# Products with v in groups of five and four key tiles, with eleven exponential buffers and three running sums

## The chip, the cores and the metric

The kernel runs on one core of a Trainium2 chip. The metric is the device time of one execution in microseconds (us), as the median of several runs. The core has a matrix engine (TensorE, PE in the rows; its weight loads are PEld), a vector engine (VectorE, DVE), a scalar engine (ScalarE, ACT), GpSimd (POOL) and a queue that issues DMAs (SyncE, SP). They run side by side and wait for each other through semaphores.

## What is computed

Attention with queries pooled in pairs, then two dense stages with their own weights. The weights come as 64-bit floats, read as pairs of integers and converted on the chip; the rest is float32.

```
q_pool = q.reshape(B, H, S // 2, 2, D).mean(axis=3)      # B, H, S, D = 4, 8, 1152, 64
scores = scale * np.matmul(q_pool, k.transpose(0, 1, 3, 2))
scores = scores - np.max(scores, axis=-1, keepdims=True)
attn = np.exp(scores)
attn = attn / (np.sum(attn, axis=-1, keepdims=True) + 1e-09)
x = np.matmul(attn, v)                                   # then (B*S/2, H*D) = (2304, 512)
h = x @ w_in;  x = (h - np.tanh(h)) @ w_out              # 512 -> 2048 -> 512
h = x @ w_in2; r = np.maximum(h, 0); out = (s * r * r + b) @ w_out2
```

## The kernel before

Heads are taken in pairs: `pairs` counts 16 of them, n = 0 to 15, four for each of the four batches, and j = 0 or 1 is the head within the pair. The 1152 keys of a head are 9 tiles of 128, t = 0 to 8. The 576 pooled queries are two halves of 288, g = 0 or 1.

For each key tile, `scores` makes two products for each half (L454 with 128 rows, L455 with 65 rows, which adds the row of maxima) into one of two PSUM buffers `s`, and ScalarE's exponential (L456) writes the half into a tile `pf` of 128 x 576. There are `PFB` buffers of `pf`. Each finished tile goes to the list `pend`. From n = 4 on, GpSimd adds the `pf` tiles of a head into a running sum `acc` (L517), two program steps after the tile is made, and when more than `BATCH` = 3 tiles are pending, `batch` multiplies the three oldest with v (L558): two halves side by side, each with 64 columns of the array, into PSUM `pv`. At the last batch of a head, one tile into the next head, `total` multiplies the running sum with ones (L572) into `su`, in the same block. The last head, (15, 1), has no running sum on GpSimd: `sum_plain` sums with ones on TensorE (L496).

A planner (the scheduler of the framework) sets the order of instructions on every engine ahead of time from priorities and its own costs; within an engine they run in that order. `batch` runs at a high priority (`AHEAD` = 400) and after the latest score product, so its products stand together in one block. Around the scores the planner puts the preparation of later pairs (transposes ptq L357, ptk L376, ptc L420; products ptm L415, whose maxima VectorE takes in L416) and the first dense stage of earlier batches (`sweep1`: h L626, y L639). These go to four PSUM buffers. During the last pair, VectorE and GpSimd also convert the weights w6 to w8 for the next stage (L215 to L239), since buffers become free there; tha and gla are VectorE's operations of the gate between h and y.

A head of nine tiles has these batches: tiles 0 to 2 when tile 3 is made, 3 to 5 at tile 6, 6 to 8 at tile 0 of the next head.

Of the kernel before, what the change touches and what calls it, by code (L numbers as in the profile page):

```python
# [46 lines left out]
GROUPS_LAST = ((0, 1, 2, 3, 4), (5, 6, 7, 8))  # L47
BATCH = 3
STORE, PUT = 8, 6
# [3 lines left out]
AHEAD = 400  # L53
PFB = 10
SOON = 40
# [8 lines left out]
def attention_moe_moe_kernel(  # L64
# [418 lines left out]

    def sum_plain(n, j, t0):


        if t0 == 0:
            return
        if (n, j) not in sums:
            sums[n, j] = psV.tile([P, HB], F32, tag="su", name=f"su{n}_{j}")  # L490
        su = sums[n, j]
        while fresh and fresh[0][:2] == (n, j) and fresh[0][2] < t0 + BATCH:
            _, _, u, pf = fresh.pop(0)
            for g in range(2):
                o = 32 * (2 * (u % 2) + g)
                mm(su[o:o + 32], ones[:, 0:32], pf[:, g * HB:(g + 1) * HB],  # L496
                   start=(u < 2), stop=(u >= NKT - 2))
        if t0 == NKT - BATCH:
            later(1, lambda: spread_plain(n, j))
# [12 lines left out]
    def add(n, j, t, r, pf):  # L512

        old = accs[n, j, r]
        if t == groups(n, j)[r][1]:
            accs[n, j, r] = ap.tile([P, SQ], F32, tag="acc", name=f"acc{n}_{j}_{r}", bufs=4)
        added[0] = pool.tensor_add(accs[n, j, r], old, pf)  # L517
# [14 lines left out]
    def finish_single(n, j):  # L532
# [12 lines left out]
        later(2, total)  # L545

    def batch():


        todo = [pend.popleft() for _ in range(BATCH)]  # L550
        n, j, t, _ = todo[0]
        if t == 0:
            pvt[n, j] = psV.tile([P, HB], F32, tag="pv", name=f"pv{n}_{j}")
        po = pvt[n, j]
        with tc.high_priority(offset=AHEAD), tc.issue_after(last[0].ins):
            for i, (_, _, u, pf) in enumerate(reversed(todo)):
                for g in (1, 0):
                    mm(po[g * D:(g + 1) * D], vos[j][:, u, 0:D], pf[:, g * HB:(g + 1) * HB],  # L558
                       start=(t == 0 and i == 0), stop=(u == NKT - BATCH))
            total()  # L560
            if plain(n, j):
                sum_plain(n, j, t)
        if t == NKT - BATCH:
            later(0, lambda: finish_head(n, j))
# [147 lines left out]
    for n in range(len(pairs)):  # L712
# [3 lines left out]
        for j in range(2):  # L716
            for t in range(NKT):
# [22 lines left out]
                else:  # L740
                    tick()
                    if len(pend) > BATCH:
                        batch()
# [363 lines left out]
```

## Time and profile before

| | us |
|---|---|
| median of 3 runs | 1344.11 |
| lowest and highest run | 1339.24, 1345.49 |
| profiled execution, device time | 1338.49 |
| span of its instructions | 1336.7 |
| TensorE busy in the span | 1307.3 (98%) |
| VectorE, ScalarE, GpSimd busy | 947.2, 634.4, 347.7 |

A row of a timeline gives start, length, engine, line, operation, result <- operands and how many records are merged; in brackets stands how long the engine was idle before it and what ended that. Records of TensorE overlap: products are pipelined, a record of 0.29 us is followed by the next start after about 0.13 us. So what a product costs the stream is the distance to the next start, not the length of its record. [...]

### The profile page before, as it was taken

How to read it: one execution, taken by the hardware profiler on the slowest of the kernel's cores; microseconds unless marked ns; L12 is line 12 of the kernel's file. 1: busy time of each engine (PE TensorE's matmuls, PEld its weight loads, DVE VectorE, ACT ScalarE, POOL GpSimd, SP SyncE). 2: the span in 40 equal slices, each digit the busy share in tenths (PEclk: the TensorE clock that was granted, in tenths of full speed). 3: DMA queues.
4: the chain of work that ended last, by engine and by line, in shares of the span. 5: the costliest groups of instructions: out<-in, count | busy, mean ns of one | idle time of the engine just before them, and what ended most of it. 6: DMA issues, size and time to landing. Idle time of an engine off the chain costs nothing.

```text
span 1336.7 us, 22381 instructions
## 1 busy us (share of the span) xinstructions
PE 1307.3 (98%) x8118; PEld 1125.2 (84%) x8118; DVE 947.2 (71%) x1888; ACT 634.4 (47%) x1527; POOL 347.7 (26%) x287
## 2 busy tenths in 40 slices
PE   6999999999999999998999999999999999999998
PEld 4777767777887777876999999999988888889887
DVE  6988885857575665668788577676878787655654
ACT  2455555555565555654333333333445454444532
POOL 0222257766677767763000000000000000000000
PEclk9999999999999999999999999999999999999999
DMA  8777766675657566443786224457434274404031
GB/s 178 160 180 179 177 153 135 143 186 133 165 112 175 129 147 156 112 119 120 239 271 193 68 82 137 147 181 245 133 118 150 95 228 153 147 0 142 1 95 48
DMA packets 203183, 191.61 MB, mean 143 GB/s; under 512 B 88640, under 2 KB 170688, under 8 KB 203072
## 3 DMA queue, kind: packets, MB, share of 16 engines
q1 hardware_dynamic: 200736, 189.59, 52.7%
q8 instruction: 64, 1.05, 0.3%
q10 hardware_dynamic: 2336, 0.59, 0.2%
q14 instruction: 47, 0.39, 0.1%
HBM read 115.34 MB, written 39.32 MB: 116 GB/s over the span
## 4 chain that ended last, share of the span: by engine, by line
PE 90%; DVE 5%; DMA 3%; ACT 1%; issue 1%; SPq 1%; POOL 0%; DVEq 0%; ACTq 0%; POOLq 0%
PE o L987 15%; PE y L828 11%; PE h L817 11%; PE pv L558 8%; PE h L1032 8%; PE s L454 6%; PE k L1032 6%; PE s L455 5%; PE ptm L415 5%; PE y L639 4%; PE h L626 3%; PE pv L526 2%; PE su L526 2%; PE ptk L376 1%; DVE mp L416 1%
## 5 line engine op out<-in xcount | busy, mean ns | idle before, releaser
L456 ACT ACTIVATE pf<-s 128x288 f32<-128x288 f32 x576 | 223.6, 410 | 161.5 <-PE s L455 156.5
L416 DVE TENSOR_REDUCE mp<-ptm 128x1 f32<-128x384 f32 x384 | 202.5, 544 | 104.5 <-PE ptm L415 100.0
L517 POOL TENSOR_TENSOR acc<-acc,pf 128x576 f32<-128x576 f32 x159 | 228.1, 1434 | 53.2 <-ACT pf L456 44.7
L454 PE MATMUL s<-U,T 128*128 128x288 f32 x576 | 191.9, 338 | 1.6 <-ACT pf L456 1.0
L455 PE MATMUL s<-U,T 65*128 65x288 f32 x576 | 172.8, 304 | 0.0
L828 PE MATMUL y<-ghb,w 128*128 128x288 f32 x784 | 171.9, 295 | 0.2 <-DVE yr L836 0.2
L817 PE MATMUL h<-xx,w 128*128 128x288 f32 x1176 | 171.0, 294 | 1.0 <-DMA xx<-x1d 0.6
L817 PEld LDWEIGHTS h<-xx,w 128*128 128x128 f32 x1176 | 160.6, 188 | 1.5 <-DMA xx<-x1d 0.9
L987 PE MATMUL o<-w,g2h 128*128 128x512 f32 x486 | 154.7, 394 | 0.0
L415 PE MATMUL ptm<-T,U 128*128 128x384 f32 x360 | 135.7, 383 | 2.7 <-DVE mp L416 1.9
L454 PEld LDWEIGHTS s<-U,T 128*128 128x128 f32 x576 | 109.9, 191 | 25.8 <-ACT pf L456 10.9
L828 PEld LDWEIGHTS y<-ghb,w 128*128 128x128 f32 x784 | 131.3, 188 | 0.4 <-DVE yr L836 0.4
L558 PE MATMUL pv<-pf,vo 128*64 128x288 f32 x864 | 120.7, 415 | 0.0
L455 PEld LDWEIGHTS s<-U,T 65*128 65x128 f32 x576 | 110.4, 192 | 7.1 <-issue 4.4
L828 PE MATMUL y<-glb,w 128*128 128x288 f32 x392 | 116.0, 296 | 0.0
L1032 PE MATMUL h<-w,w 128*128 128x384 f32 x522 | 107.4, 339 | 0.0
L1032 PEld LDWEIGHTS h<-w,w 128*128 128x128 f32 x522 | 93.6, 188 | 9.4 <-DVE w L902 1.1
L987 PEld LDWEIGHTS o<-w,g2h 128*128 128x128 f32 x486 | 89.7, 187 | 10.0
L987 PE MATMUL o<-w,g2l 128*128 128x512 f32 x234 | 92.6, 396 | 0.0
L558 PEld LDWEIGHTS pv<-pf,vo 128*64 128x64 f32 x864 | 55.6, 136 | 41.0 <-issue 10.8
L950 ACT ACTIVATE r_c<-r_c 128x384 f32<-128x384 f32 x72 | 37.8, 524 | 109.5 <-DVE r_c L1044 53.1
L955 DVE SCALAR_TENSOR_TENSOR g2l<-r_c,sb,g2h 128x384 fp32r<-128x384 f32 x96 | 59.1, 616 | 39.7 <-ACT g2h L954 39.4
(145 smaller groups left out, 2369.4 us busy)
## 6 DMA issues: line engine op xcount, KB each, us to landing
xx<-x1d SPq DMA_DIRECT2D x80, 288.0 KB
T<-T SPq DMA_DIRECT2D x50, 288.0 KB
raw<-in_moe_w_in_dram SPq DMA_DIRECT2D x23, 512.0 KB
raw<-in_moe_w_out_dram SPq DMA_DIRECT2D x23, 512.0 KB
qr<-in_q_dram SPq DMA_DIRECT2D x32, 288.0 KB
vo<-in_v_dram SPq DMA_DIRECT2D x32, 288.0 KB
x1d<-xo SPq DMA_DIRECT2D x64, 144.0 KB
kr<-in_k_dram SPq DMA_DIRECT2D x30, 288.0 KB
```

What stands on the lines that cost most here:

```text
L415: mm(pt, U1[j][:, q0:q0 + P], T1[j][:, kk], start=True, stop=True)
L416: newest[0] = dve.reduce_max(mp[:, s, i:i + 1], pt, axis=AX.X)
L454: last[0] = mm(ps, T1[j][:, t * P:(t + 1) * P], U1[j][:, sl], start=True, stop=False)
L455: last[0] = mm(ps, T2[j][:, t * P:(t + 1) * P], U2[j][:, sl], start=False, stop=True)
L456: act(pf[:, sl], ps, AF.Exp, scale=SCALE)
L517: added[0] = pool.tensor_add(accs[n, j, r], old, pf)
L558: mm(po[g * D:(g + 1) * D], vos[j][:, u, 0:D], pf[:, g * HB:(g + 1) * HB], start=(t == 0 and i == 0), stop=(u == NKT - BATCH))
L817: mm(ps[:, :n], w[:, a, c * P:(c + 1) * P], xx[:, c, x, 0:n], start=(i == 0 and c == 0), stop=(i == 2 and c == NDC - 1))
L828: mm(ys[i][c], w[:, a, c * P:(c + 1) * P], x, start=(f == fa and r == 0), stop=(f == fb - 1 and r == 2))
L955: gates.append(dve.scalar_tensor_tensor(out=gl, in0=r, scalar=sb2[:, 1:2], in1=f32(gh), op0=ALU.add, op1=ALU.subtract))
L987: mm(os[r], g[:, k * P:(k + 1) * P], w[a], start=(first and n == half and x == 0), stop=(last and n != half and x == 2))
L1032: mm(ps, u[a][:, (2 * wa + c) * P:(2 * wa + c + 1) * P], xs[b][xa][:, c], start=(fresh_ and h == 0 and c == 0), stop=(h == 2 and c == 1), ...
```

## The change

`BATCH` is replaced by `SPLIT` = (5, 4): a head's tiles 0 to 4 are multiplied with v when tile 5 is made, tiles 5 to 8 at tile 0 of the next head. The last head keeps three threes (`SPLIT_LAST`). `PFB` goes from 10 to 11, and the running sums from 4 buffers to 3, each of the same size, so the memory in use is the same. The sums over keys in the last head are unchanged.

```
-BATCH = 3
+SPLIT = (5, 4)
+SPLIT_LAST = (3, 3, 3)
-PFB = 10
+PFB = 11
...
-            accs[n, j, r] = ap.tile([P, SQ], F32, tag="acc", name=f"acc{n}_{j}_{r}", bufs=4)
+            accs[n, j, r] = ap.tile([P, SQ], F32, tag="acc", name=f"acc{n}_{j}_{r}", bufs=3)
...
+    def size(n, j, t):
+
+        split = SPLIT_LAST if plain(n, j) else SPLIT
+        return split[[sum(split[:i]) for i in range(len(split))].index(t)]
+
     def batch():
-        todo = [pend.popleft() for _ in range(BATCH)]
-        n, j, t, _ = todo[0]
+        n, j, t, _ = pend[0]
+        todo = [pend.popleft() for _ in range(size(n, j, t))]
+        closing = todo[-1][2] == NKT - 1
...
-                       start=(t == 0 and i == 0), stop=(u == NKT - BATCH))
+                       start=(t == 0 and i == 0), stop=(closing and i == len(todo) - 1))
...
-                    if len(pend) > BATCH:
+                    if len(pend) > size(*pend[0][:3]):
                         batch()
```

The planner makes new orders of all engines from this. In TensorE's order the products with v and the sums behind them stand in 72 unbroken blocks before and in 49 now. Right behind a block stands a ptc transpose 4 times before and 18 times now. Line numbers of the changed kernel are higher by 1 ahead of `batch` and by 7 behind it.

The score product of a half k+2 writes the buffer of half k. How many other products (not scores) stand between half k's last product and half k+2's first, in attention from pair 4 on, is this:

| other products between | 0 | 1 | 2 | 3 | 4 or more | a block with v |
|---|---|---|---|---|---|---|
| places before | 15 | 10 | 39 | 64 | 168 | 132 |
| places now | 36 | 22 | 50 | 54 | 180 | 86 |

TensorE around the first block of head (7, 1), before: s is a score product, pv a product with v, h the first dense stage, ptm a maximum's product.

```order
L626 MATMUL h0_1_2_3699<-xx0_1_3522,w2_152 128x288
L454 MATMUL s7_1_3_0_3748<-U1_1_1_179,T1_1_1_173 128x288
L455 MATMUL s7_1_3_0_3748<-U2_1_195,T2_1_169 128x288
L415 MATMUL ptm8_0_3_0_3752<-T1_2_0_174,U1_2_0_180 128x384
L626 MATMUL h0_1_2_3699<-xx0_1_3522,w2_152 128x288
L454 MATMUL s7_1_3_1_3756<-U1_1_1_179,T1_1_1_173 128x288
L455 MATMUL s7_1_3_1_3756<-U2_1_195,T2_1_169 128x288
L558 MATMUL pv7_1_3765<-pf7_1_2_3723,vo1_191 64x288 x2
L558 MATMUL pv7_1_3765<-pf7_1_1_3701,vo1_191 64x288 x2
L558 MATMUL pv7_1_3765<-pf7_1_0_3662,vo1_191 64x288 x2
L626 MATMUL h0_1_2_3699<-xx0_1_3522,w2_152 128x288
L415 MATMUL ptm8_0_3_1_3761<-T1_2_0_174,U1_2_0_180 128x384
```

Now, the same head's first block, on TensorE:

```order
L455 MATMUL s7_1_4_1_3778<-U1_1_1_179,T1_1_1_173 128x288
L456 MATMUL s7_1_4_1_3778<-U2_1_195,T2_1_169 128x288
L455 MATMUL s7_1_5_0_3805<-U1_1_1_179,T1_1_1_173 128x288
L456 MATMUL s7_1_5_0_3805<-U2_1_195,T2_1_169 128x288
L455 MATMUL s7_1_5_1_3817<-U1_1_1_179,T1_1_1_173 128x288
L456 MATMUL s7_1_5_1_3817<-U2_1_195,T2_1_169 128x288
L565 MATMUL pv7_1_3833<-pf7_1_4_3766,vo1_191 64x288 x2
L565 MATMUL pv7_1_3833<-pf7_1_3_3747,vo1_191 64x288 x2
L565 MATMUL pv7_1_3833<-pf7_1_2_3723,vo1_191 64x288 x2
L565 MATMUL pv7_1_3833<-pf7_1_1_3701,vo1_191 64x288 x2
L565 MATMUL pv7_1_3833<-pf7_1_0_3660,vo1_191 64x288 x2
L421 MATMUL ptc8_0_3785<-ident_75,m8_0_3634 5x128
```

The block comes two tiles later and is longer, the score products ahead of it stand next to each other, and a ptc transpose has moved right behind it.

GpSimd near the end of head (15, 0), before: acc is the running sum, w the subtraction that ends a weight's conversion.

```order
L239 TENSOR_TENSOR w6_7439<-t0_6_0_0_7442,w6_7439 128x256
L239 TENSOR_TENSOR w6_7439<-t0_6_0_1_7462,w6_7439 128x256
L517 TENSOR_TENSOR acc15_0_1_7498<-pf15_0_5_7450,pf15_0_6_7470 128x576
L517 TENSOR_TENSOR acc15_0_1_7498<-acc15_0_1_7498,pf15_0_7_7509 128x576
L239 TENSOR_TENSOR w7_7440<-t0_7_0_0_7501,w7_7440 128x256
L517 TENSOR_TENSOR acc15_0_1_7498<-acc15_0_1_7498,pf15_0_8_7532 128x576
```

Now, GpSimd at the same place:

```order
L518 TENSOR_TENSOR acc15_0_1_7496<-pf15_0_5_7443,pf15_0_6_7474 128x576
L240 TENSOR_TENSOR w6_7432<-t0_6_0_0_7435,w6_7432 128x256
L240 TENSOR_TENSOR w6_7432<-t0_6_0_1_7466,w6_7432 128x256
L518 TENSOR_TENSOR acc15_0_1_7496<-acc15_0_1_7496,pf15_0_7_7507 128x576
L518 TENSOR_TENSOR acc15_0_1_7496<-acc15_0_1_7496,pf15_0_8_7530 128x576
L240 TENSOR_TENSOR w7_7433<-t0_7_0_0_7499,w7_7433 128x256
```

The last addition, of tile 8, has moved ahead of the subtraction for w7.

VectorE at the end of the last head, before: t and raw are the last weight's conversion, ri and xv the last head's division, tha and gla the last gate of the sweep.

```order
L215 TENSOR_SCALAR t0_8_1_1_7764<-raw0_8_1_1_7720 128x256
L218 SCALAR_TENSOR_TENSOR t0_8_1_1_7764<-raw0_8_1_1_7720,t0_8_1_1_7764 128x256
L592 RECIPROCAL ri15_1_7819<-ri15_1_7819 128x144
L221 SCALAR_TENSOR_TENSOR t0_8_1_1_7764<-raw0_8_1_1_7720,t0_8_1_1_7764 128x256
L224 TENSOR_SCALAR raw0_8_1_1_7720<-raw0_8_1_1_7720 128x256
L592 RECIPROCAL ri15_1_7819<-ri15_1_7819 128x144
L227 SCALAR_TENSOR_TENSOR t0_8_1_1_7764<-raw0_8_1_1_7720,t0_8_1_1_7764 128x256
L653 TENSOR_TENSOR tha2_1_4_7873<-h2_1_4_7801,tha2_1_4_7873 128x288
L597 TENSOR_TENSOR xv15_1_7823<-xv15_1_7823,ri15_1_7819 128x288
L657 TENSOR_TENSOR gla2_1_4_7877<-tha2_1_4_7873,gha2_1_4_7876 128x288
```

Now, VectorE at the same place:

```order
L216 TENSOR_SCALAR t0_8_1_1_7764<-raw0_8_1_1_7720 128x256
L660 TENSOR_TENSOR tha2_1_4_7873<-h2_1_4_7801,tha2_1_4_7873 128x288
L219 SCALAR_TENSOR_TENSOR t0_8_1_1_7764<-raw0_8_1_1_7720,t0_8_1_1_7764 128x256
L604 TENSOR_TENSOR xv15_1_7823<-xv15_1_7823,ri15_1_7819 128x288
L222 SCALAR_TENSOR_TENSOR t0_8_1_1_7764<-raw0_8_1_1_7720,t0_8_1_1_7764 128x256
L225 TENSOR_SCALAR raw0_8_1_1_7720<-raw0_8_1_1_7720 128x256
L664 TENSOR_TENSOR gla2_1_4_7877<-tha2_1_4_7873,gha2_1_4_7876 128x288
L228 SCALAR_TENSOR_TENSOR t0_8_1_1_7764<-raw0_8_1_1_7720,t0_8_1_1_7764 128x256
```

Both reciprocals now stand further ahead, tha ahead of four operations of the conversion, and gla behind three of them. At the start of the same stretch, tha2_1_0 now stands ahead of the two casts of w6, which stood ahead of it before. In SyncE's order the load of the last weight part, raw0_8_1_1, now stands behind the first load of xx0, the next stage's input, instead of ahead of it.

## Rows read from the trace of the kernel before

**Rows 1.** Busy time by engine, 183 to 626 us: stretch, length, then each engine's.

```profile
183.00:626.00 443.00, 436.23 (x2969) 337.68 (x2968) 291.95 (x567) 248.13 (x675) 309.46 (x238) 1.00 0.60 141
```

**Rows 2.** Groups by line, 183 to 626 us: count, busy us, mean ns, idle before.

```profile
L454 PE MATMUL s<-U,T 128*128 128x288 f32 x426 | 136.2, 323 | 1.6 <-ACT pf L456 1.0
...
L558 PE MATMUL pv<-pf,vo 128*64 128x288 f32 x864 | 120.7, 415 | 0.0
```

**Rows 3.** Timeline of TensorE around two blocks with v: start, length.

```profile
500.07 0.29 PE L455 MATMUL s<-U,T 65*128 65x288 f32 x1
500.29 1.68 PE L558 MATMUL pv<-pf,vo 128*64 128x288 f32 x12
501.89 0.44 PE L415 MATMUL ptm<-T,U 128*128 128x384 f32 x1
502.17 0.29 PE L454 MATMUL s<-U,T 128*128 128x288 f32 x1
502.30 0.30 PE L455 MATMUL s<-U,T 65*128 65x288 f32 x1
502.44 0.34 PE L415 MATMUL ptm<-T,U 128*128 128x384 f32 x1
502.62 0.29 PE L639 MATMUL y<-gha,w 128*128 128x288 f32 x1
...
515.69 1.68 PE L558 MATMUL pv<-pf,vo 128*64 128x288 f32 x12
...
517.78 0.44 PE L415 MATMUL ptm<-T,U 128*128 128x384 f32 x1
```

**Rows 4.** Timeline of TensorE, ptc right behind a block.

```profile
219.19 0.27 PE L420 MATMUL ptc<-ident,m 128*4 128x128 f32 x1
219.22 0.38 PE L626 MATMUL h<-xx,w 128*128 128x288 f32 x1
219.43 0.29 PE L454 MATMUL s<-U,T 128*128 128x288 f32 x1
```

**Rows 5.** Timeline of TensorE, the products behind a ptc in the open.

```profile
503.72 0.43 PE L415 MATMUL ptm<-T,U 128*128 128x384 f32 x1
503.98 0.41 PE L357 MATMUL ptq<-ident,qr 96*128 96x96 f32 x3
```

**Rows 6.** Timeline of TensorE, score products close together.

```profile
442.01 0.29 PE L639 MATMUL y<-gha,w 128*128 128x288 f32 x1
442.15 0.40 PE L454 MATMUL s<-U,T 128*128 128x288 f32 x1
442.38 0.29 PE L455 MATMUL s<-U,T 65*128 65x288 f32 x1
442.51 0.38 PE L454 MATMUL s<-U,T 128*128 128x288 f32 x1
442.73 0.30 PE L455 MATMUL s<-U,T 65*128 65x288 f32 x1
443.18 0.40 PE L454 MATMUL s<-U,T 128*128 128x288 f32 x1 [0.15 <-ACT pf L456]
443.42 0.30 PE L455 MATMUL s<-U,T 65*128 65x288 f32 x1
```

**Rows 7.** Waits of ScalarE, 183 to 626 us: in total, times, longest.

```profile
ACT pf L456 <- PE s L455: 106.4, 178, 2.4
```

**Rows 8.** Busy time by engine, 597.5 to 631 us, columns as in rows 1.

```profile
597.50:631.00 33.50, 29.91 (x211) 21.36 (x210) 31.60 (x71) 15.45 (x44) 14.40 (x16) 0.95 0.48 146
```

**Rows 9.** Timeline of TensorE in the last pair: its waits.

```profile
606.87 0.72 PE L572 MATMUL su<-acc,ones 128*64 128x288 f32 x4 [1.95 <-POOL acc L517]
...
631.39 0.40 PE L639 MATMUL y<-gha,w 128*128 128x288 f32 x1 [1.75 <-ACT gha L656]
632.19 0.40 PE L639 MATMUL y<-gla,w 128*128 128x288 f32 x1 [0.40 <-DVE gla L657]
```

**Rows 10.** Timeline of GpSimd in the last pair: the subtraction for w7.

```profile
604.54 0.74 POOL L239 TENSOR_TENSOR w<-t,w 128x256 fp32r<-128x256 f32 x1 [1.85 <-PE pv L558]
```

More of the change, by code (lines that the diff above doesn't have):

```diff
@@ L482, in attention_moe_moe_kernel, with sum_plain @@
     sums = {}
-    def sum_plain(n, j, t0):
+    def sum_plain(n, j, t0, t1):
         if t0 == 0:
@@ L491, in sum_plain @@
         su = sums[n, j]
-        while fresh and fresh[0][:2] == (n, j) and fresh[0][2] < t0 + BATCH:
+        while fresh and fresh[0][:2] == (n, j) and fresh[0][2] < t1:
             _, _, u, pf = fresh.pop(0)
@@ L497, in sum_plain @@
                    start=(u < 2), stop=(u >= NKT - 2))
-        if t0 == NKT - BATCH:
+        if t1 == NKT:
             later(1, lambda: spread_plain(n, j))
@@ L558, in batch @@
                     mm(po[g * D:(g + 1) * D], vos[j][:, u, 0:D], pf[:, g * HB:(g + 1) * HB],
-                       start=(t == 0 and i == 0), stop=(u == NKT - BATCH))
+                       start=(t == 0 and i == 0), stop=(closing and i == len(todo) - 1))
             total()
             if plain(n, j):
-                sum_plain(n, j, t)
-        if t == NKT - BATCH:
+                sum_plain(n, j, t, todo[-1][2] + 1)
+        if closing:
             later(0, lambda: finish_head(n, j))
```

## The prediction

> **What bounds the kernel now.** I read the busy time by stage first. Attention with the first sweeps, 183 to 626 us, keeps TensorE busy for 436.23 of 443 us [rows 1]; the two dense stages behind it hold no instruction that the change touches. So inside this stretch a term counts if it is time of TensorE's stream, or a wait of that stream, and other engines count through such waits. Next the groups of lines: the products with v are 864 records, 120.7 us [rows 2]. [...] Third, the timeline around one batch, for what entering and leaving it costs [rows 3], and around runs of score products, for what waiting on ScalarE's exponentials costs [rows 6]. Last, the end of the stretch, where another engine takes over [rows 8 to 10].
>
> **The change, part by part.** *Fewer blocks.* Before a block, the last score product starts at 500.07 and the block at 500.29: 0.22, where the same product is left after 0.14 at 502.30. That is 0.08 more. The block holds TensorE from 500.29 to 501.89, 1.60; one with four more records for the running sum holds it from 515.69 to 517.78, 2.09, so two more steps of a pair cost 0.49, six steps 1.47, and 0.13 is extra. The ptm product behind the block holds TensorE from 501.89 to 502.17, 0.28, where the one at 502.44 takes 0.18: 0.10 more [rows 3]. Together 0.31 per block, with starts rounded to 0.01; I take 0.33, since two differences are rounded down here. The order has 72 blocks before and 49 now, 23 fewer: 23 x 0.33 = 7.6 us less on TensorE's stream. The products themselves stay the same in number.
>
> *Neighbours.* A ptc transpose in the open makes the next product slow: 503.72 to 503.98 is 0.26 for a ptm that else takes 0.18 [rows 5]. Right behind a block the two dearer exits become one: from ptc at 219.19 the next product starts 0.03 later and is left after 0.21, 0.08 over its usual 0.13 [rows 4], and the 0.10 behind the block is not paid. 4 ptc products stood so, now 18: 14 x 0.10 = 1.4 us less.
>
> *Scores closer together.* This is the term that decides. There are two PSUM buffers for scores, so the product of half k+2 waits for the exponential of half k. With longer blocks there are fewer of them to stand between score products, and the order shows the scores bunched between blocks. Where nothing stands between but half k+1, the start comes 0.45 after the last one, 442.73 to 443.18, against 0.13 undisturbed, and the product is left after 0.24 instead of 0.13: 0.42 in all. Where two other products stand between, as ahead of 442.51, the product starts in time but is left after 0.22 instead of 0.13, so 0.09 to 0.10 [rows 6]. The number of places with none or one between rises from 25 to 58, with two from 39 to 50, with three it falls from 64 to 54. The nearest prices are 0.10 and 0.42; for none or one I take 0.25 (not every such place waits fully: the score products' mean length is 323 ns, against 0.29 to 0.30 undisturbed [rows 2, 3], which over 426 of them is about 12 us of waiting in all), for two 0.10, for three 0.07 (0.10 at 442.15, at many others nothing). That is 33 x 0.25 + 11 x 0.10 - 10 x 0.07 = 8.7 us more. Bounds: all at the lower price 33 x 0.10 + 0.4 = 3.7; all at the upper 33 x 0.42 + 11 x 0.24 = 16.5.
>
> *Buffers.* ScalarE's exponentials wait for score products, 106.4 us in 178 waits; no wait of it for GpSimd, which would be one for a free buffer, is among the view's rows [rows 7]. The eleventh buffer is there because a tile now stays until two tiles later; three running sums suffice, since at most two heads have one open, and the last pair three. I cost both at nothing; the cover is about three tiles of slack per buffer, and if it were gone an exponential would wait for a block to end, up to 1.60 us [rows 3].
>
> *The last pair.* Here three queues move. On GpSimd the weight subtraction w7 waited 1.85 us for the block of products with v and stood ahead of the last addition of head (15,0); TensorE waited 1.95 us for that addition at 606.87 [rows 9, 10]. Now both additions stand ahead of it, so that wait should shrink to under 0.5. But this saves little: from 597.5 to 631 VectorE is busy 31.60 of 33.50 us [rows 8], converting weights between the gate's subtractions, and TensorE waits at the end for what VectorE hands over: 1.75 us at 631.39 and 0.40 at 632.19 [rows 9]. An earlier TensorE waits longer there. What counts is VectorE's own order: tha2_1_4 now stands ahead of four operations of the last conversion, but two casts of w6 moved behind tha2_1_0, into the busy stretch, and gla2_1_4 now has three conversion operations between it and tha2_1_4. These nearly cancel for tha and put gla about 1 us later. On SyncE one of the last weight loads now stands behind a load of the next stage that waits for the last products with v. I take 1 us more, between 2 less (the wait at 631.39 gone) and 2 more (it doubles).
>
> **Sum.** -7.6 - 1.4 + 8.7 + 1.0 = +0.7 us, against the profiled execution's own 1338.5 us, so 1339.2. The median of the runs shown, 1344.1, lies 5.6 us above that execution; the difference carried to the median gives 1344.8, and I write 1345.
>
> **The rivals.** *The gain is kept* (0.18). The waits for exponentials don't grow: a bunch only moves waits that came anyway, since ScalarE is idle for over 100 us waiting for scores [rows 7] and has room. For it: most places wait by less than 0.15. Against it: the price is the latency of a product, an exponential and the two hand-overs, which room on ScalarE doesn't shorten. Then the sum is -7.6 - 1.4 and a tail between 0 and -2: 1344.1 - 9 = 1335, down to 1333. *The bunches cost the full price* (0.17), slower: each of the 33 new close places waits 0.42, because the bunches are runs of four to six halves ahead of a block, as in head (7,1), where each wait meets the next. -9.0 + 16.5 + 1 = +8.5: 1352.6. With the places with two between at 0.24, the kernel is slower by over 0.5% (6.7 us) from a mean of 0.37 per new close place on: -9.0 + 1 + 2.6 + 33 x 0.37 = 6.8. The Trainium skill has a rule on this side: TensorEngine Tiling (Array Packing), section Performance Considerations, says that packing the array speeds up TensorE but not the emptying of PSUM, which may then bound. Here the rows of the scores agree that PSUM is waited for, in part; by that rule alone the time would be this rival's. *The change doesn't do what it says* (0.02): the planner could have split the groups again; the order shows 49 unbroken blocks, so this is all but out, and would give 1344.
>
> **How the numbers follow.** My forecast, gains and waits about equal, has 0.63 and reaches from 1338 to 1350. The runs before spread over 6 us, so under 0.5%, 6.7 us, a measurement of this kernel can hardly be told from no change. Below 1337.4 lies the first rival, 0.18; above 1350.8 the second and a little of the forecast's upper end, 0.19; within, 0.63. To leave out no more than 2 in 10 the range reaches half into each rival: 1336 to 1353.
>
> **What would show it.** In the trace after, the products with v should stand in blocks of 20 and 16 records, 46 of them in 23 heads, with the entering and leaving of [rows 3]; and the busy time of the line falls from 120.7 to about 116 us. The mean length of the score product with 128 rows rises from 323 ns towards 335 to 340; if it stays at 323 the first rival holds, at 355 and more the second. TensorE's wait for the running sum near 605 falls below 0.5 us, and the wait ahead of the last y products stays at 2 us or grows: if it vanishes, the tail is not VectorE's, and the kernel gains 3 us on my sum. Waits of the exponential for GpSimd would show that eleven buffers are too few.

## The result, and the profile after

| | before | after |
|---|---|---|
| median of 17 runs, us | 1345.22 | 1351.73 |
| lowest and highest run | 1338.06, 1350.36 | 1346.35, 1362.67 |
| profiled execution, device time | 1338.49 | 1350.46 |

The ratio of the times is 1.0069, with a 95% interval of 1.0050 to 1.0088: the change makes the kernel slower by 0.7%, 9.3 us (6.7 to 11.8). The forecast was 1345, no change; the range of 1336 to 1353 holds the time, its upper end just so. The two profiled executions differ by 12.0 us, more than the runs do, since the one of before is among the fastest of its kernel.

The busy time of each engine over the whole span of the kernel after, the first part of its page:

```profile
PE 1313.3 (97%) x8118; PEld 1132.2 (84%) x8118; DVE 951.7 (71%) x1888; ACT 635.0 (47%) x1527; POOL 345.6 (26%) x287
```

The other engines do what they did before, to 5 us. TensorE is busy for 6 us more, in a span that is 12 us longer, though it computes the same products. The stretch with attention by windows, columns as in [rows 1], of after and then of before up to 12 us earlier:

```profile
183.00:652.00 469.00, 453.29 (x3043) 354.70 (x3042) 302.16 (x579) 252.72 (x684) 310.29 (x241) 0.98 0.59 138
```

```profile
183.00:640.00 457.00, 448.09 (x3053) 348.96 (x3052) 297.70 (x579) 252.27 (x685) 312.22 (x241) 1.00 0.60 141
```

15.7 us of 469 are idle on TensorE, where 8.9 of 457 were, and the granted clock, the third number from the right, is 0.98 and not 1.00. Next the groups of TensorE's lines, 183 to 640 us, with the columns of [rows 2]:

```profile
L455 PE MATMUL s<-U,T 128*128 128x288 f32 x426 | 139.6, 331 | 6.5 <-ACT pf L457 4.8
...
L565 PE MATMUL pv<-pf,vo 128*64 128x288 f32 x864 | 118.2, 419 | 0.0
```

The products with v fell from 120.7 to 118.2 us and not to the 116 that was forecast. The score product's mean length rose by only 8 ns, from 323 to 331, but its idle time before rose too, from 1.6 to 6.5: together 3.4 + 4.9 = 8.3 us on this line alone. The waits of the weight loads and of the products in the same stretch say what it waited for (total, times, longest):

```profile
PEld s L455 <- ACT pf L457: 19.0, 58, 2.3
...
PE s L455 <- ACT pf L457: 4.8, 17, 2.0
PE ptq L358 <- DVE mp L417: 2.8, 1, 2.8
```

Before, the first of these was 8.5 us in 29 waits and the second 1.0 in 6:

```profile
PEld s L454 <- ACT pf L456: 8.5, 29, 0.5
...
PE s L454 <- ACT pf L456: 1.0, 6, 0.3
```

**Where the stream's time went.** To add this up, I took TensorE's products in order, from the start of pair 4 to the first of the dense stage behind attention. For each kind of product and successor the undisturbed distance of starts is the median over places where nothing waits; the sum of these is called work below. What a distance is longer by goes to one cause: to half clock if the granted clock is about 0.5 there, else to the scores if one of the two products is a score product, to the four shared buffers if it is a transposition or a ptm product, to the end if it lies behind the last block with v. The remainder (blocks, sums, h and y) is small. All in us, one trace each; the same work was sized 428.2 to 431.3 in kernels with the same 72 blocks, so a difference of 3 us in that column says little.

| kernel | total | work | scores | shared buffers | half clock | end | rest |
|---|---|---|---|---|---|---|---|
| before | 462.3 | 431.3 | 16.4 | 6.9 | 1.6 | 3.3 | 2.8 |
| after | 475.5 | 421.1 | 27.6 | 11.9 | 9.0 | 4.4 | 1.6 |
| difference | +13.2 | -10.2 | +11.2 | +5.0 | +7.4 | +1.1 | -1.2 |

So the saved blocks are there in full, the scores' waits take them back, and two things that my sum didn't have make the loss.

The split is softer than its decimals. With medians taken over all thirteen traces together, work differs by about -6 instead of -10.2, and scores and shared buffers together by about +13 instead of +16.2; the distances around the blocks, further below, speak for some -9 of work. The longest wait for a shared buffer, 2.79 us, comes right behind a score product, so by the rule above it counts as scores. And the idle time of TensorE that VectorE ended, ahead of transpositions and ptm products, is 3.6 us after and 3.2 before, 183 to 640 us: one long wait instead of several short ones, so most of the +5.0 is not seen as such waits. Of the +7.4, half clock itself can be no more than 6.8, half of the 13.7 us by which its stretches grew (17.1 after, 3.4 before); the rest is waiting that fell into them.

Matched product by product, after lags before by 0.2 us at the start of pair 4, 6.2 at the start of head (15, 0), 8.2 at (15, 1), 8.3 at the end of the last block with v, 13.4 where the dense stage begins and 12.3 at its end. About 5 us of the loss therefore come behind the last block.

**The scores' waits and the clock in one place.** TensorE's timeline ahead of a block of five tiles, after:

```profile
448.27 0.40 PE L455 MATMUL s<-U,T 128*128 128x288 f32 x1 [0.16 <-ACT pf L457]
448.51 0.29 PE L456 MATMUL s<-U,T 65*128 65x288 f32 x1
448.64 0.37 PE L455 MATMUL s<-U,T 128*128 128x288 f32 x1
448.85 0.29 PE L456 MATMUL s<-U,T 65*128 65x288 f32 x1
449.31 0.40 PE L455 MATMUL s<-U,T 128*128 128x288 f32 x1 [0.16 <-ACT pf L457]
...
450.35 0.46 PE L455 MATMUL s<-U,T 128*128 128x288 f32 x1 [0.17 <-ACT pf L457]
450.60 0.45 PE L456 MATMUL s<-U,T 65*128 65x288 f32 x1
...
451.45 3.87 PE L565 MATMUL pv<-pf,vo 128*64 128x288 f32 x20
455.25 0.27 PE L421 MATMUL ptc<-ident,m 128*4 128x128 f32 x1
```

From 448.27 to 450.35 four halves of scores take 2.08 us, 0.52 for a half, where two undisturbed products take 0.27. It is the pattern of [rows 6], repeated until the block comes. Then at 450.60 all lengths grow, and the block of 20 records takes 3.87 us. The same block at full clock, at another place of the same timeline:

```profile
237.86 2.65 PE L565 MATMUL pv<-pf,vo 128*64 128x288 f32 x20
```

The windows on either side of 450.6 (columns as in [rows 1]):

```profile
447.20:450.60 3.40, 2.91 (x15) 2.02 (x14) 2.82 (x6) 2.83 (x8) 2.84 (x3) 0.99 0.54 132
450.60:454.00 3.40, 3.40 (x16) 1.90 (x17) 0.00 (x0) 1.17 (x4) 3.24 (x3) 0.51 1.07 213
```

The granted clock goes from the upper of its two levels (2.4 GHz) to the lower (1.2 GHz) for 3.4 us, behind a stretch in which TensorE had short waits and was busy for 2.91 of 3.40 us. At half speed 3.4 us do the work of 1.7, so such a stretch costs 1.7 us. Between pair 4 and the dense stage the trace of before has one, at 607.4; after has 17 us of them, at 245.8, 450.6, 600.7 and 641.7 (the last twice as long). The one at 600.7 stands, as here, in a run of score products ahead of a block.

The runs bear this out. Each has its mean granted clock over the whole execution on record. The median is 0.993 in the 17 runs of after. Beside each other on one chip it is 0.997 in 32 runs of before, 0.993 in 9 runs of a kernel with the order of after (the old buffers, below) and 0.996 in 12 runs with the scores spread. By estimate, 0.004 of some 1350 us is 5.4 us, more than half of the loss.

**A shared buffer.** TensorE's timeline near 241 us, after, and VectorE's timeline beside it:

```profile
241.61 0.29 PE L455 MATMUL s<-U,T 128*128 128x288 f32 x1
244.69 0.47 PE L358 MATMUL ptq<-ident,qr 96*128 96x96 f32 x3 [2.79 <-DVE mp L417]
```

```profile
238.79 1.96 DVE L219 SCALAR_TENSOR_TENSOR t<-raw,t 128x256 int32<-128x256 int32 x2
240.67 1.01 DVE L222 SCALAR_TENSOR_TENSOR t<-raw,t 128x256 int32<-128x256 int32 x1
241.61 1.49 DVE L225 TENSOR_SCALAR raw<-raw 128x256 int32<-128x256 int32 x1
243.02 0.41 DVE L222 SCALAR_TENSOR_TENSOR t<-raw,t 128x256 int32<-128x256 int32 x1
...
244.09 1.01 DVE L417 TENSOR_REDUCE mp<-ptm 128x1 f32<-128x384 f32 x2
```

The transposition needs one of the four shared buffers, and the buffer holds a ptm product whose maximum VectorE takes only at 244.09, behind a weight's conversion, here two of them nearly in a row. Before, the maxima stood between the conversion's operations, as this part of VectorE's timeline of before shows:

```profile
238.94 0.91 DVE L221 SCALAR_TENSOR_TENSOR t<-raw,t 128x256 int32<-128x256 int32 x1
239.77 0.55 DVE L416 TENSOR_REDUCE mp<-ptm 128x1 f32<-128x384 f32 x1
240.24 1.03 DVE L224 TENSOR_SCALAR raw<-raw 128x256 int32<-128x256 int32 x1
...
241.76 0.54 DVE L416 TENSOR_REDUCE mp<-ptm 128x1 f32<-128x384 f32 x1
```

TensorE's longest wait there was 0.76 us:

```profile
241.89 0.44 PE L415 MATMUL ptm<-T,U 128*128 128x384 f32 x1 [0.76 <-DVE ql L366]
```

Behind the wait of 2.79 us the clock of after went down as well; the windows ahead of 245.8 and behind it:

```profile
242.40:245.80 3.40, 1.11 (x9) 1.07 (x10) 3.40 (x10) 0.60 (x3) 1.27 (x2) 0.99 0.62 154
245.80:249.20 3.40, 3.40 (x16) 3.24 (x15) 2.42 (x7) 2.52 (x7) 1.53 (x2) 0.51 0.63 157
```

**The end.** TensorE's waits in the last pair and behind it, after:

```profile
614.53 0.71 PE L579 MATMUL su<-acc,ones 128*64 128x288 f32 x4 [0.93 <-POOL acc L518]
...
618.53 0.40 PE L455 MATMUL s<-U,T 128*128 128x288 f32 x1 [2.02 <-ACT pf L457]
...
641.57 0.51 PE L646 MATMUL y<-gha,w 128*128 128x288 f32 x1 [2.65 <-ACT gha L663]
643.24 0.61 PE L646 MATMUL y<-gla,w 128*128 128x288 f32 x1 [1.16 <-DVE gla L664]
```

Against [rows 9] the wait for the running sum shrank from 1.95 to 0.93, and those for gha and gla grew from 1.75 and 0.40 to 2.65 and 1.16. The wait at 618.53 is 2.02, where before the longest such wait in the last pair was 0.26 (622.06). ScalarE's timeline says why: its exponential stood behind gha, which waited for VectorE's tha.

```profile
617.11 0.44 ACT L663 ACTIVATE gha<-tha 128x288 fp32r<-128x288 f32 x1 [5.44 <-DVE tha L660]
...
618.08 0.70 ACT L457 ACTIVATE pf<-s 128x288 f32<-128x288 f32 x2
```

### The profile page after: what moved, and what is told of

Its sections match the earlier page's. It is cut to its first block, busy times and chain, and to the rows that moved or that the text cites. A ratio compares the mean times of both kernels' runs of the same rounds, so it can differ in the third digit from the quotient of the medians.

```text
span 1348.6 us, 22343 instructions
## 1 busy us (share of the span) xinstructions
PE 1313.3 (97%) x8118; PEld 1132.2 (84%) x8118; DVE 951.7 (71%) x1888; ACT 635.0 (47%) x1527; POOL 345.6 (26%) x287
## 4 chain that ended last, share of the span: by engine, by line
PE 86%; DVE 6%; DMA 3%; ACT 3%; issue 2%; POOL 1%; SPq 0%; DVEq 0%; ACTq 0%; POOLq 0%
PE o L994 15%; PE h L824 11%; PE y L835 11%; PE h L1039 8%; PE pv L565 7%; PE k L1039 6%; PE s L455 6%; PE s L456 5%; PE ptm L416 4%; PE y L646 4%; PE h L633 3%; PE pv L527 2%; PE su L527 2%; ACT pf L457 2%; PE ptk L377 1%
## 5 line engine op out<-in xcount | busy, mean ns | idle before, releaser
L455 PE MATMUL s<-U,T 128*128 128x288 f32 x576 | 195.3, 344 | 6.5 <-ACT pf L457 4.8
L565 PE MATMUL pv<-pf,vo 128*64 128x288 f32 x864 | 118.2, 419 | 0.0
L565 PEld LDWEIGHTS pv<-pf,vo 128*64 128x64 f32 x864 | 58.7, 139 | 43.5 <-issue 10.9
```

The costliest lines, as they stand in the source:

```text
L455: last[0] = mm(ps, T1[j][:, t * P:(t + 1) * P], U1[j][:, sl], start=True, stop=False)
```

## The experiments

The theory to test is that the kernel lost by its score products standing close together, so that the saved blocks are given back as waits. Its rivals: the buffers (eleven and three instead of ten and four), the order at the end alone, a lack of score buffers that a third one would mend, and the four shared buffers that VectorE empties. Each kernel was timed beside runs of the kernel before on the same chip; the ratio is to these.

The planner counts how much work of the dense sweep to put between the scores; MOE_NS is that amount per step. The first kernel sets it higher, which spreads the scores; the second does the same to the kernel before.

**More sweep work between the scores, groups of five and four** (from the kernel after):

```
-MOE_NS = 445
+MOE_NS = 460
```

> Groups of five and four, with 460 instead of 445 ns of first-stage work offered per tile (MOE_NS), which changes the planner's order alone: 49 blocks as in the change, but places with none or one other product between two uses of a score buffer fall from 58 to 26 (before: 25) and with two from 50 to 42 (before: 39), and no run of more than five score halves. Theory A (the loss is the close places and what follows from them): the saved blocks come through, 6 to 10 us faster than before, ratio 0.993 to 0.996. Theory B (longer blocks cost by themselves, whatever stands around them): as slow as the change, ratio 1.004 to 1.009. Theory C (the loss sits in the last pair's tail, some 4 us of it): part of the gain only, ratio 0.996 to 1.000.

Measured: 1342.21 us, ratio 0.9992 (0.9968 to 1.0016). The order has 49 blocks as after, but 26 places with none or one product between two halves, where before has 25 and after 58.

**The same in threes** (from the kernel before):

```
-MOE_NS = 445
+MOE_NS = 460
```

> The kernel before, threes, with the same 460 instead of 445: the control for the number itself. 72 blocks, places with none or one between 13 (before 25), with two 33 (before 39). Theory A: 12 fewer close places at about 0.25 us and 6 at 0.13, some 3 to 4 us faster, ratio 0.996 to 0.999. Theory B and C: as before, ratio 0.999 to 1.001. If this is as fast as the first run of this call, the gain there is the number's and not the blocks'.

Measured: 1340.04 us, ratio 0.9986 (0.9965 to 1.0007), with 13 such places.

With the scores apart, the whole loss is gone, so the groups of five are not slow in themselves. That the closeness alone is the cause is not shown by it, since the number changes the order as a whole. Of the 10.5 us by which this kernel's stream is shorter than that of after (the table below), 3.9 come behind the last block with v, where VectorE's order at the end sets the time; and its stretches at half clock are 10.2 us instead of 17.1. But nothing is won either. The waits for scores in the first of these kernels, 183 to 640 us, are near those of before:

```profile
PEld s L455 <- ACT pf L457: 11.7, 42, 1.1
```

**Groups of five and four with the old buffers** (from the kernel after):

```
-PFB = 11
+PFB = 10
-... tag="acc", name=f"acc{n}_{j}_{r}", bufs=3)
+... tag="acc", name=f"acc{n}_{j}_{r}", bufs=4)
```

> Groups of five and four with ten exponential buffers and four running sums, as before; TensorE's order is the same as in the change, row by row. Theory A: buffers play no part, as the change, ratio 1.005 to 1.009. Theory D (fewer running sums or their places in memory cost): most of the loss goes, ratio below 1.003. If ten buffers are too few, exponentials wait for GpSimd or TensorE and the ratio rises above 1.009.

Measured: 1352.87 us, ratio 1.0067 (1.0044 to 1.0090), with the same order on TensorE as after. The buffers play no part. It is also a second trace of the same order, and shows how far one trace can be trusted: total 472.5 us (475.5 after), scores 27.4 us (27.6 after), shared buffers 11.5 (11.9), half clock 5.8 (9.0).

**The last pair in threes** (from the kernel after):

```
-        split = SPLIT_LAST if plain(n, j) else SPLIT
+        split = SPLIT_LAST if n == len(pairs) - 1 else SPLIT
```

> The change with threes in both heads of the last pair instead of the last head alone (50 blocks; places with none or one between 54). If the tail's loss of about 4 us in the change comes from the groups in head (15,0), it goes: ratio 1.002 to 1.005. If it comes from what the planner does in the last head anyway, or from TensorE arriving later, it stays: ratio 1.005 to 1.009.

Measured: 1346.19 us, ratio 1.0029 (1.0007 to 1.0051). The two intervals touch, but the trace agrees that the end is back as it was. TensorE's waits in its last pair:

```profile
618.06 0.71 PE L579 MATMUL su<-acc,ones 128*64 128x288 f32 x4 [1.92 <-POOL acc L518]
633.29 0.40 PE L455 MATMUL s<-U,T 128*128 128x288 f32 x1 [0.33 <-ACT pf L457]
642.67 0.40 PE L646 MATMUL y<-gha,w 128*128 128x288 f32 x1 [1.78 <-ACT gha L663]
643.47 0.61 PE L646 MATMUL y<-gla,w 128*128 128x288 f32 x1 [0.40 <-DVE gla L664]
```

They are those of [rows 9] to some hundredths. So of the 0.7% about 0.4%, some 5 us, belong to the order of the last pair, though only the head (15, 0) is split differently there; about 0.3% remain. Against the run with the old buffers, timed with it and with the order of after, it is 6.7 us.

**Both** (from the kernel after):

```
-MOE_NS = 445
+MOE_NS = 465
...
-        split = SPLIT_LAST if plain(n, j) else SPLIT
+        split = SPLIT_LAST if n == len(pairs) - 1 else SPLIT
```

> Groups of five and four, 465 ns of first-stage work per tile instead of 445, and threes in both heads of the last pair: the two parts of the loss found so far taken away together. 50 blocks; places with none or one product between 27, with two 33 (before 25 and 39). If the close places and the tail are the whole loss, the 22 saved blocks show: 5 to 9 us faster than before, ratio 0.993 to 0.997. If a third part remains (waits for the four shared PSUM buffers that VectorE empties, some 6 us more than before in both kernels with groups of five), 1 us faster to 2 us slower than before, ratio 0.998 to 1.002.

Measured: 1343.62 us, ratio 0.9990 (0.9966 to 1.0014). No better than with the sweep work alone. The gain of 8 us of work that these kernels still have isn't seen in the time. The table below says where most of it stays, and the end takes the rest. Counted from the start of pair 4, this kernel's trace is 3.7 us ahead of before at the last block with v, and 0.5 behind it where the dense stage begins; the threes with more sweep work are 2.9 ahead and then 1.4 behind. In both, TensorE comes early and waits for VectorE's tha; here, and then in the threes:

```profile
636.01 0.61 PE L646 MATMUL y<-gha,w 128*128 128x288 f32 x1 [5.09 <-DVE tha L660]
```

```profile
629.76 0.61 PE L639 MATMUL y<-gha,w 128*128 128x288 f32 x1 [4.70 <-DVE tha L653]
```

It is what the prediction says of the last pair: an earlier TensorE waits longer there.

**A third score buffer, taken from the shared ones, groups of five and four** (from the kernel after):

```
-    psP = ... name="psP", bufs=4, space=PSUM))
-    psS = ... name="psS", bufs=2, space=PSUM))
+    psP = ... name="psP", bufs=3, space=PSUM))
+    psS = ... name="psS", bufs=3, space=PSUM))
```

> The change with three PSUM buffers for scores and three shared ones, instead of two and four. A score product then waits for the half three before it. Theory A: the score waits (32 us before pair 15's end in the change) fall to under 10, while the shared buffers' waits grow; set against the same step in the kernel before (next run), the change is faster by the saved blocks, 5 to 9 us. Theory E (longer blocks bunch VectorE's work too, and the shared buffers' waits are worth as much as the score waits): the change stays slower than its control, by 3 us or more.

Measured: 1355.09 us, ratio 1.0089 (1.0058 to 1.0120).

**The same edit in threes** (from the kernel before):

```
-    psP = ... name="psP", bufs=4, space=PSUM))
-    psS = ... name="psS", bufs=2, space=PSUM))
+    psP = ... name="psP", bufs=3, space=PSUM))
+    psS = ... name="psS", bufs=3, space=PSUM))
```

> The kernel before with three PSUM buffers for scores and three shared ones: the control of the run before this one. Score waits fall from 21 us to under 8 and the shared buffers' waits grow; by how much the two outweigh each other is open, 0.99 to 1.02 of the kernel before.

Measured: 1349.03 us, ratio 1.0034 (1.0011 to 1.0056). TensorE's weight loads in the groups with three score buffers, 183 to 640 us:

```profile
PEld ptm L416 <- DVE mp L417: 13.5, 22, 3.4
PEld s L455 <- ACT pf L457: 6.8, 21, 1.9
```

The third buffer does take the scores' waits away, 6.8 us of 19.0 are left. But with three shared buffers TensorE now waits for VectorE's maxima, and the kernel is no faster. The groups stay 0.55% behind the threes under the same edit: the waits have moved to the next scarce buffer and not gone. These two runs change more than the buffers: counted in the traces, the planner left 134 places with none or one product between with groups and 100 in threes, where two score buffers had 58 and 25.

**Half of each maximum, groups of five and four** (from the kernel after; VectorE reads half of the columns, the other half is left out):

```
-                    newest[0] = dve.reduce_max(mp[:, s, i:i + 1], pt, axis=AX.X)
+                    newest[0] = dve.reduce_max(mp[:, s, i:i + 1], pt[:, :KB // 2], axis=AX.X)
```

> The change with each maximum in the later products' reduction (L417) taken over half of its columns, which shortens 384 operations of VectorE from 0.55 us to about 0.3 and leaves out that part of the maximum (the softmax does not depend on it). The planner's order then has 25 places with none or one between and 41 with two, as few as before. Theory E: with VectorE relieved, the shared buffers' waits go, and the saved blocks show: 8 us or more faster than the kernel before. Theory A without E: 2 to 8 us faster, from the places alone.

Measured: 1349.04 us, ratio 1.0033 (1.0004 to 1.0061).

**The same edit in threes** (from the kernel before):

```
-                    newest[0] = dve.reduce_max(mp[:, s, i:i + 1], pt, axis=AX.X)
+                    newest[0] = dve.reduce_max(mp[:, s, i:i + 1], pt[:, :KB // 2], axis=AX.X)
```

> The kernel before, but VectorE takes each maximum over half of the columns only (the other half is left out), as in the changed kernel of the run before this one, which came to 1.0033 of the kernel before. If the waits for the four shared buffers, which VectorE empties, are a cost of the groups of five alone, the threes have little to get back: 0.998 to 1.000, about 1344 us, and the gap between groups and threes halves to about 0.4%. If the shorter maxima help both alike, this is 0.995 to 0.997, about 1340 us, the gap stays at 0.6 to 0.7%, and VectorE's maxima say nothing on why the groups of five lose.

Measured: 1342.62 us, ratio 1.0012 (0.9989 to 1.0034). The threes gain nothing by it, the groups about 0.4%, as if VectorE's time were a cost of the groups alone. The pair doesn't settle it: the planner, too, knows that the maxima are shorter, and made a new order with 25 close places instead of 58 in the groups, so that the gain may be the spreading of the first experiment again. In threes the places fell too, from 25 to 12 by the trace. What VectorE's maxima cost the groups by themselves stays open.

**One group of nine** (from the kernel after), to see whether gain and loss both grow:

```
-SPLIT = (5, 4)
+SPLIT = (9,)
```

> The changed kernel with all nine tiles of a head in one block (the last head keeps its threes): 26 blocks instead of 49, 98 places with none or one product between two halves of scores instead of 58. By the terms measured so far, 23 blocks less at 0.34 us are 7.8 us off, and 33 more places with none between at 0.26, 7 with one at 0.19, and some 16 with two or three at 0.10 to 0.15 are about 12 us on: 4 us over the groups of five and four, about 1356 us, 1.010 of the kernel before. If waits for shared buffers and stretches at half clock grow with the bunches too, another 4 to 8 us: 1360 to 1364, 1.013 to 1.016. If the saved blocks decide, 1.001 or less. Here an exponential needs the buffer of the tile 11 before it, two tiles of slack; if that is too little, ScalarE shows waits for GpSimd or for products with v that the groups of five don't have.

Measured: 1369.65 us, ratio 1.0216 (1.0172 to 1.0260).

**One group of nine, twelve buffers and two running sums:**

```
-PFB = 11
+PFB = 12
-... tag="acc", name=f"acc{n}_{j}_{r}", bufs=3)
+... tag="acc", name=f"acc{n}_{j}_{r}", bufs=2)
```

> As the run with one group of nine, with twelve buffers for exponentials and two running sums instead of eleven and three: the same order on TensorE. If slack in the buffers costs nothing in the group of nine, the same time within 0.3%. If eleven are too few there, this one is faster by the waits that the run with eleven shows; if two running sums are too few, GpSimd's first addition of a head waits for TensorE's sum and this one is slower.

Measured: 1368.77 us, ratio 1.0200 (1.0164 to 1.0237): the same, so it isn't the slack of the buffers. The loss is beyond all three of my expectations. Waits of TensorE with one group of nine, 183 to 640 us, and the longest of them in its timeline:

```profile
PEld s L455 <- ACT pf L457: 25.4, 73, 1.5
...
PE ptm L416 <- DVE mp L417: 5.2, 3, 4.5
```

```profile
243.05 0.30 PE L456 MATMUL s<-U,T 65*128 65x288 f32 x1
247.88 0.69 PE L416 MATMUL ptm<-T,U 128*128 128x384 f32 x1 [4.54 <-DVE mp L417]
```

It is the place at which after waits 2.79 us, and longer, but not for the same reason alone. VectorE's maximum stands behind a conversion here too, and this conversion waited 6.28 us for the DMA of its weights, as VectorE's timeline shows; the run with twelve buffers shows the same 6.28.

```profile
243.75 1.10 DVE L216 TENSOR_SCALAR t<-raw 128x256 int32<-128x256 int32 x1 [6.28 <-DMA raw<-in_moe_w_out_dram]
```

The stream of TensorE, split as above, for all of them:

| kernel | total | work | scores | shared buffers | half clock | end |
|---|---|---|---|---|---|---|
| groups, more sweep work | 465.0 | 423.0 | 18.3 | 12.3 | 4.7 | 3.5 |
| threes, more sweep work | 463.7 | 429.7 | 15.1 | 10.2 | 2.3 | 5.5 |
| groups, old buffers | 472.5 | 421.1 | 27.4 | 11.5 | 5.8 | 5.3 |
| groups, last pair in threes | 471.2 | 421.5 | 24.9 | 11.8 | 7.3 | 3.2 |
| groups, more work and last pair | 462.8 | 423.0 | 19.3 | 10.0 | 3.7 | 5.9 |
| groups, three score buffers | 475.3 | 420.9 | 16.6 | 24.1 | 6.6 | 4.7 |
| threes, three score buffers | 468.9 | 428.2 | 9.7 | 17.9 | 4.8 | 5.1 |
| groups, half maxima | 463.5 | 421.2 | 23.7 | 10.0 | 3.2 | 4.0 |
| threes, half maxima | 460.8 | 428.6 | 15.9 | 8.5 | 3.1 | 3.5 |
| one group of nine | 485.0 | 415.5 | 40.4 | 15.2 | 6.4 | 2.6 |
| nine, twelve buffers | 490.7 | 415.5 | 40.0 | 14.5 | 14.2 | 2.5 |

From 72 to 49 to 26 blocks the work falls by 10.2 and 15.8 us, and the scores' waits rise by 11.2 and 24.0, those for shared buffers by 5.0 and 8.3 (the group of nine against before, in both). The gain grows with the blocks saved, and the loss faster; a part of the loss with nine is the wait for that DMA, 4.54 us on TensorE. In the two kernels with groups and more sweep work the scores wait some 2 to 3 us more than before, and shared buffers and half clock take 3 to 5 and 2 to 3 us more, which is what the blocks save and 2 us more in the one, about the same in the other.

One wait belongs to the groups whatever the scores do. All seven traces with groups of five and four hold a wait of TensorE for VectorE's maxima of 2.8 to 3.4 us that ends between 244.7 us (after) and 256.5, and a stretch at half clock that begins during it or within 2 us behind it. In the four traces in threes the longest wait in that place is 0.8 to 1.4 us, and one of them has such a stretch. The spread scores leave this wait as it is, and the halved maxima too (3.42).

No kernel here is clearly faster than the one before: the best, the threes with more sweep work, is at 0.9986 with 1 in its interval.

## Why the prediction was wrong

*Fewer blocks and their neighbours: right.* The forecast was -7.6 - 1.4 = -9.0 us; the stream's work fell by 10.2, and by 15.8 for 46 blocks, 0.34 for each, against 0.33. The two views ahead of it, [rows 3] and [rows 4], were enough. The distances of starts agree without the split: a score product ahead of a block is left after 0.09 us more than else, blocks of 12 and 20 records take 1.61 and 2.58 us, so that 8 records take 0.97 and 0.15 is extra, and a ptm product behind a block takes 0.10 more (medians over the traces). That is 0.34. The neighbours show as well. Behind a block stand 18 ptc transposes in after and none with one group of nine, so by the prediction's prices the step from 49 to 26 blocks should be worth 7.6 - 1.8 = 5.8 us, and work fell by 5.6. The line of products with v fell by 2.5 us and not by 4 to 5, since two blocks in the half-clock stretches last 3.87 and 4.07 us and not 2.65.

*Scores closer together: the mechanism right, the size too small.* The term was 8.7 with bounds of 3.7 and 16.5; 11.2 was measured (11.0 in the kernel with the old buffers). By the class of place, the mean wait in the traces of before and after was this, in us:

| other products between | 0 | 1 | 2 | 3 |
|---|---|---|---|---|
| my price | 0.25 | 0.25 | 0.10 | 0.07 |
| before | 0.22 | 0.24 | 0.13 | 0.07 |
| after | 0.26 | 0.19 | 0.15 | 0.10 |

My 0.25 was fair. I was low on the many places with two or three between, whose price I had from single rows: by the table they added 3.4 us, and I had 0.4. Their price also rose, perhaps since a bunch makes the exponentials late for the next places too; no run shows that by itself. The view that I named as a test, the mean length of the score product, told only part: it came to 331 ns, below the 335 to 340 forecast, while most of the growth stood as idle time ahead of the product.

*Buffers at nothing: right*, by the two runs that change them alone.

*What was left out: the step that failed.* The prediction priced the score buffers and took all else in the new order to cost what it had cost. Its opening says that other engines count through the waits of TensorE's stream, but for the four shared buffers no wait was looked for, and the clock was not in the sum at all: both stood at nothing without a reason. They came to +5.0 and +7.4 us in the traces (+4.6 and +4.2 with the old buffers), while all that the sum had came to +0.9 (-10.2 + 11.2 + 1.1 - 1.2) against its +0.7. That this agrees so well is luck in part, since the gain was 1.2 larger and the scores' waits 2.5 larger than forecast. Of the two, the clock is the firmer, some 5 us by the runs' granted clock; the shared buffers' part rests on the split, but for the one wait of 2.79 us and the stretch at half clock behind it. The shared buffers' part can be seen beforehand only in the order: in the stretch near 240 us two conversions stood ahead of the maxima on VectorE. I had compared VectorE's order at the end of the last head alone.

*The last pair: the direction right, the size wrong.* I took +1.0, between -2 and +2. The stretch between the last block with v and the dense stage lengthened from 13.4 to 18.5 us, and putting the pair back in threes gave about 5 us back. The wait for the running sum fell, to 0.93 and not under 0.5; the waits for gha and gla rose by 1.66, inside my bound. The other part is the stretch at half clock of 6.8 us at 641.7, behind those waits, 3.4 us of time by the estimate above. The 2.02 us at 618.53, where ScalarE's exponential stood behind gha, cost nothing on balance: from the start of (15, 1) to the last block with v the lag went from 8.2 to 8.3 us, since before had its wait of 1.95 us and its stretch at half clock there. The prediction did not ask what stands on ScalarE behind a gate that waits for VectorE.

*The rival that came nearest.* "The bunches cost the full price" gave 1352.6, 0.9 us from the median, by another sum: it had +16.5 for the scores, and 11.2 were measured; the rest came from what no case contained. That the number fits is no proof of it. A rule of the Trainium skill stood on that rival's side (TensorEngine Tiling (Array Packing), section Performance Considerations: packing speeds up TensorE, not the emptying of PSUM, which may then bound). The runs agree with its direction: what is gained on TensorE by larger groups, 10.2 us, is lost to waits for PSUM buffers, 11.2 for the scores' alone.

*The chances.* I gave 0.19 to slower by over 0.5%. The cases of the sum were balanced, but all unknown costs that I had left at nothing could only be losses: a new order on an engine that was busy for 98% can wait more, hardly less.

What stays open: whether the waits alone bring the clock down, what the closeness of the scores costs without the new order at the end and on VectorE, and what the shared buffers' waits cost without the closeness. No run here holds one of them fixed while changing the other.

## What to carry to other kernels

Fewer switches between shapes of products are worth what the timeline says, here 0.34 us each, but on an engine that is hardly idle the products that now stand next to each other must be priced against the buffers that they reuse; all of the buffers, the shared ones too. Where a planner makes the order anew, compare the whole of it, on the engines that empty those buffers first of all, since a wait shows up wherever its order got worse. And add the idle time before a group to its length before calling its cost small. Where the stretch ends in a wait for another engine, as here for VectorE's gate, time won ahead of it is not won.

## What the runs showed of the hardware

- The granted clock went down to its lower level for 3.4 us, in some places for 6.8 or 10.2, behind stretches in which TensorE had waited: after 1.11 us of work in 3.40 (at 245.8), but also after 2.91 in 3.40 with only short gaps (at 450.6). TensorE's windows around the wait of 2.65 us at the end:

```profile
638.20:641.70 3.50, 0.85 (x7) 0.62 (x5) 3.50 (x9) 0.86 (x2) 0.69 (x1) 1.00 0.86 270
641.70:648.50 6.80, 5.64 (x23) 5.32 (x24) 2.42 (x5) 1.57 (x4) 2.00 (x3) 0.50 0.29 72
```

  It isn't the same in every execution: the two traces of the order of after hold 17 and 14 us of it between pair 4 and the dense stage, the two of the order with one group of nine 17 and 31.
- All three traces that hold the wait of 2.79 us hold a stretch at half clock with it: 1.1 us behind its end in after, 1.9 behind it with the old buffers, and during it with the last pair in threes. By estimate a stretch of 3.4 us costs 1.7 more. That the wait is the reason is not shown. Most of the 58 waits for scores had no such stretch behind them.
- A conversion's operation on VectorE took 1.01 us at 240.67 and 0.41 at 243.02, the same line and the same shape. No run tests why.
- The time at which TensorE reaches pair 4 differs by up to 9 us between executions (176.2 in the trace of before, 185.4 in those with half maxima), from the first 56 us, which the changes don't touch. It may be much of the scatter of the runs, and is the reason why the streams above are compared from pair 4 on.
